# Reading the moving operand of float32r matmuls in pairs of columns 128 apart

## The chip, the cores and the metric

The kernel runs on one core of a Trainium2 chip. The metric is the device time of one execution in microseconds. The profile is one execution taken by the hardware profiler; its times are counted from the first instruction's start.

## The reference

A linear attention feeds a two-layer network, all in float32. Batch 8, 8 heads, sequence 576, head width 64, so 4608 tokens of width 512; the inner width of the network is 2048.

```python
kv  = np.einsum('bhsd,bhse->bhde', k, v)
o   = np.einsum('bhsd,bhde->bhse', q, kv)
rms = np.sqrt(np.mean(o * o, axis=-1, keepdims=True) + 1e-06)
x   = (o / rms * g_norm).transpose(0, 2, 1, 3).reshape(4608, 512)
h   = x @ w_in                                   # 4608 x 2048
g   = 0.5 * h * (1.0 + erf(h / np.sqrt(2.0)))
out = g @ w_out                                  # 4608 x 512
```

The weights w_in and w_out arrive as float64 and are handed over as 64-bit words.

## The kernel before

The tokens are worked through in nine chunks of 512. In every chunk the attention output x stands transposed, features on the partitions and tokens along the free dimension; layer 1 gives h transposed in the same way, and layer 2 takes the Gelu of it as stationary operand, so that its output has tokens on the partitions and the 512 features of the result along the free dimension.

To keep float32 precision with float32r matmuls, each operand is split into a high part (rounded to float32r) and the low rest, and a product is made of three matmuls: high by high, low by high, high by low. A float32r matmul has a stationary operand of 128 x 128 and a moving one of 256 or 512 columns; each loads its stationary operand first.

Chunks 0 and 1 are done plainly. `layer1` (L680) makes 12 matmuls of 512 columns for each of the 16 blocks of 128 inner features; the first two blocks of chunk 0 are plain float32 matmuls of 256 columns (L670) because their split weights aren't ready. `layer2` (L707) makes 12 matmuls of 512 columns for each block. In the same time VectorE and ScalarE turn the 64-bit words of the weights into split float32r parts (`top_w`, L635; `bits_w`, L645 and L648; `high_w`, L656; `low_w`, L660), form sums of weight blocks, and store these to HBM.

Chunks 2 to 8 use a fast scheme with seven products of half-sized blocks in the place of eight, for both layers. `product` (L569) makes six matmuls of 256 columns for one product of layer 1, and 56 products in a chunk; `Fast.matmuls` (L1257) makes 12 matmuls of 256 columns for each of 28 ticks of layer 2. Weight sums come back from HBM through a ring of six tiles (`RING`, `fetch`, L513 and L518): the tile is fetched again as soon as its last matmul has read it, and a fetch holds the operands of 12 matmuls. Some sums stay resident.

Queries of the next chunk are projected by plain float32 matmuls with 64 x 64 weights (`project_pair`, L243), four or more for each pair of heads, between the other matmuls of TensorE. `sum_squares` (L836) belongs to the first chunk alone: it streams 64 columns of a table against 128-column stationary blocks in plain float32. All instruction order is written out by hand. SyncE's queue issues the transfers.

In the code before, the moving operands are adjacent columns in memory. The pieces of them, in `product`, `layer1`, `layer2` and `Fast.matmuls`:

```python
rhs=x[:, z, kb]
rhs=at.block((p // 2, half))[:, p % 2]
rhs=at.x[p][:, x]
rhs=parts["out", i][:, w]
rhs=y
```

`finish` is defined and called from nowhere.

Of the kernel before, what the change touches and what calls it, by code (L numbers as in the profile page):

```python
# [8 lines left out]
F32 = mybir.dt.float32  # L9
F32R = mybir.dt.float32r  # L10
I32 = mybir.dt.int32
AF = mybir.ActivationFunctionType
ALU = mybir.AluOpType
# [3 lines left out]
P = 128  # L17
EPS = 1e-6
CH = 512
# [5 lines left out]
HALF = CH // 2  # L25
# [12 lines left out]
def linear_attn_rms_gelu_ffn(  # L38
# [16 lines left out]
    nc = tc.nc  # L55
    ctx.enter_context(tc.manual_schedule())
    NT, DM = out.shape
    B, NP = kv_main.shape[:2]
    S = NT // B
    NJ = kv_main.shape[3] // (2 * P)  # L60
    TAIL = kv_tail.shape[1]
    D = g_norm.shape[0]
# [6 lines left out]
    work = ctx.enter_context(tc.tile_pool(name="work", bufs=1))  # L69
# [4 lines left out]

    def bank(name):
        return psum.tile([P, 512], F32, name=name)

    turn = {"h": 0, "a": 0}

    def next_bank(kind):  # L80

        turn[kind] ^= 1
        return bank(f"{kind}{turn[kind]}")

    kv = [const.tile([P, NP, 2, D], F32, name=f"kv{s}") for s in range(2)]
# [91 lines left out]
    def rows(r):  # L177
        return slice(r * D, (r + 1) * D)
# [26 lines left out]
    class Attn:  # L205
# [22 lines left out]
        def project_pair(self, p):  # L228


            q = self.q.pop(p).rearrange("p (h n) -> p h n", h=2)
            parts = []
            for half in range(2):
                a, t = 0, self.t0 + half * HALF
                while a < HALF:
                    b = (t + a) // S
                    e = min(HALF, (b + 1) * S - t)
                    parts.append((a, e, half, b))
                    a = e
            for a, e, half, b in sorted(parts):  # L240
                ps = self.ps[p // 2, half]
                for h in range(2):
                    nc.tensor.matmul(  # L243
                        out=ps[rows(h), p % 2 * HALF + a:p % 2 * HALF + e],
                        lhsT=kv[b % 2][rows(half), p, h ^ half], rhs=q[rows(half), h, a:e],
                        start=True, stop=True,
                    )

# [313 lines left out]
    def product(at, j, k, out, first=False):  # L562
        *key, n = place_in(j, k)
        key = tuple(key)
        w, x = operand(at.c, key)[n], at.x[k]
        for kb in range(2):
            hi, lo = (w[:, m * HALF + kb * P:m * HALF + (kb + 1) * P] for m in range(2))
            for i, (y, z) in enumerate(((hi, 0), (lo, 0), (hi, 1))):
                nc.tensor.matmul(  # L569
                    out=out, lhsT=y, rhs=x[:, z, kb], start=first and kb + i == 0,  # L570
                    stop=kb == 1 and i == 2, skip_group_check=True,
                )
        if (n == 1) or (k == 6 and j == NJ2 - 1):
            used(at.c, key)
# [40 lines left out]
    raw, parts = {}, {}  # L615
# [49 lines left out]
    def layer1(at, i):  # L665
        h = next_bank("h")
        if at.c == 0 and i < FULL:
            for half in range(2):
                for p in range(NP):
                    nc.tensor.matmul(  # L670
                        out=h[:, half * HALF:(half + 1) * HALF],
                        lhsT=ws[i].bitcast(F32)[:, p * P:(p + 1) * P],
                        rhs=at.block((p // 2, half))[:, p % 2],
                        start=(p == 0), stop=(p == NP - 1),
                    )
            return h
        order = ((HI, 0), (LO, 0), (HI, 1))
        for m, (w, x) in enumerate(order):
            for p in range(NP):
                nc.tensor.matmul(  # L680
                    out=h, lhsT=parts["in", i][:, w][:, p * P:(p + 1) * P], rhs=at.x[p][:, x],
                    start=(m + p == 0), stop=(m == 2 and p == NP - 1),
                )
        return h
# [17 lines left out]
    def layer2(acc, blocks, closed=None):  # L702
        for t, ps in enumerate(acc):
            ts = slice(t * P, (t + 1) * P)
            for (gh, gl), i in blocks:
                for m, (x, w) in enumerate(((gh, HI), (gh, LO), (gl, HI))):
                    nc.tensor.matmul(  # L707
                        out=ps, lhsT=x[:, ts], rhs=parts["out", i][:, w],
                        start=(i == 0 and m == 0),
                        stop=(m == 2 and (i == NF - 1 or (i, t) == (closed, CH // P - 1))),  # L710
                    )

    def finish(acc, blocks, t0):


        layer2(acc[:-1], blocks)
        store(acc[:-1], t0)
        t = len(acc) - 1
        ts, rows = slice(t * P, (t + 1) * P), slice(t0 + t * P, t0 + (t + 1) * P)
        rest_ps = next_bank("h")  # L720
        for half in range(2):
            ps = rest_ps[:, :HALF] if half else acc[t][:, :HALF]
            n = 0
            for (gh, gl), i in blocks:
                for x, w in ((gh, 0), (gh, DM), (gl, 0)):
                    w += half * HALF
                    n += 1
                    nc.tensor.matmul(
                        out=ps, lhsT=x[:, ts], rhs=parts["out", i][:, w:w + HALF],
                        start=(half == 1 and n == 1), stop=(n == 3 * len(blocks)),  # L730
                        skip_group_check=True,
                    )
            o = work.tile([P, DM], I32, name="wz"[half], bufs=2).bitcast(F32)[:, :HALF]
            if half:
                nc.vector.tensor_copy(out=second_half, in_=acc[t][:, HALF:])
                nc.vector.tensor_tensor(out=o, in0=ps, in1=second_half, op=ALU.add)
            else:
                second_half = work.tile([P, CH], F32, name="sq")[:, :HALF]
                nc.scalar.copy(out=o, in_=ps)
            nc.sync.dma_start(out=out[rows, half * HALF:(half + 1) * HALF], in_=o)  # L740

    def store(acc, t0, both=True, to=None):
        for t, ps in enumerate(acc):
            if to is None:
                o = work.tile([P, DM], I32, name="wz"[t % 2], bufs=2).bitcast(F32)
            else:
                o = to[:, t]
            if both and not t % 2:
                nc.vector.tensor_copy(out=o, in_=ps)
            else:  # L750
                nc.scalar.copy(out=o, in_=ps)
            nc.sync.dma_start(out=out[t0 + t * P:t0 + (t + 1) * P, :], in_=o)
# [3 lines left out]
    first, second = attn[:2]  # L756
# [44 lines left out]
    for d in range(0, 2 * D, BLK):  # L801
        h = d // D * D
        nc.gpsimd.tensor_tensor(
            out=fold[:, d:d + BLK], in0=ident[:, h:h + BLK], in1=ident[:, h + BLK:h + 2 * BLK],
            op=ALU.add,
        )
    SQ = ("sq", "gh", "gl", "gh")
    sq, NG = {}, CH // P
# [23 lines left out]
    def sum_squares(n):  # L832
# [9 lines left out]
    ps = next_bank("a")  # L842
    nc.tensor.matmul(out=ps[:, :1], lhsT=g_row, rhs=heads[:1, :1], start=True, stop=True)
    nc.vector.tensor_scalar(
        out=half_g, in0=ps[:, :1], scalar1=0.5, scalar2=None, op0=ALU.mult
# [3 lines left out]
        out=sums[:, :P], lhsT=ones, rhs=eps, start=True, stop=False,  # L849
        skip_group_check=True,  # L850
# [3 lines left out]
        out=root_g, in0=half_g, scalar1=D ** 0.5, scalar2=None, op0=ALU.mult  # L854
# [9 lines left out]
    for half in range(2):  # L864
# [6 lines left out]
        out=sums[:, :n_fold].rearrange("p (g b) -> p g b", g=2), lhsT=fold,  # L871
# [22 lines left out]
    for half in range(2):  # L894
# [6 lines left out]
        n = 2 + half  # L901
# [296 lines left out]
    class Fast:  # L1198
# [44 lines left out]
        def matmuls(self, i, sides=(0, 1)):  # L1243
            k, n = self.ticks[i]
            name = self.BANKS[k]
            two = self.c == NCH - 1 and name == "a0"
            if k in (0, 2, 1) and n == 0 and 0 in sides:
                self.bank[name] = [bank(name), bank("a1")] if two else [bank(name)] * 2
            w = operand(self.c, ("out", k, n))
            slot, op = self.ops[i]  # L1250
            for p in range(2):
                hi, lo = (op[:, z * CH + p * HALF:z * CH + (p + 1) * HALF] for z in range(2))
                wh, wl = (w[p][:, m * HALF:(m + 1) * HALF] for m in range(2))
                for a in sides:
                    at = slice(a * P, (a + 1) * P)
                    for m, (x, y) in enumerate(((hi, wh), (hi, wl), (lo, wh))):
                        nc.tensor.matmul(  # L1257
                            out=self.bank[name][a][:, a * HALF:(a + 1) * HALF],
                            lhsT=x[:, at], rhs=y,
                            start=(k in (0, 2, 1) and n + p + m == 0 and (two or a == 0)),  # L1260
                            stop=(n == GROUPS - 1 and p == 1 and m == 2), skip_group_check=True,
                        )
            if 1 in sides:
                used(self.c, ("out", k, n))
                free.append(slot)
                self.ops.pop(i)
# [208 lines left out]
```

## Time and profile before

| what | value |
|---|---|
| time, median of 3 runs | 772.47 us (771.27 to 773.56) |
| span of the profiled execution, first to last instruction | 769.2 us |
| TensorE busy | 762.4 us, 99% of the span |
| VectorE, ScalarE, GpSimd busy | 75%, 48%, 20% |
| DMA | 244.90 MB, 318 GB/s mean |

The time of a run lies 2.1 to 4.4 us above the span of the profiled execution, since it takes in what stands before the first and after the last instruction; the profiled execution itself has no other time than its span. A matmul's duration in the profile is that from its start until its last result, and starts follow one another before the one ahead has ended; the pace of a run of matmuls is the distance of their starts.

### The profile page before, as it was taken

How to read it: one execution, taken by the hardware profiler on the slowest of the kernel's cores; microseconds unless marked ns; L12 is line 12 of the kernel's file. 1: busy time of each engine (PE TensorE's matmuls, PEld its weight loads, DVE VectorE, ACT ScalarE, POOL GpSimd, SP SyncE). 2: the span in 40 equal slices, each digit the busy share in tenths (PEclk: the TensorE clock that was granted, in tenths of full speed). 3: DMA queues.
4: the chain of work that ended last, by engine and by line, in shares of the span. 5: the costliest groups of instructions: out<-in, count | busy, mean ns of one | idle time of the engine just before them, and what ended most of it. 6: DMA issues, size and time to landing. Idle time of an engine off the chain costs nothing.

```text
span 769.2 us, 16747 instructions
## 1 busy us (share of the span) xinstructions
PE 762.4 (99%) x6558; PEld 721.4 (94%) x6558; DVE 575.8 (75%) x1056; ACT 369.4 (48%) x722; POOL 156.3 (20%) x140
## 2 busy tenths in 40 slices
PE   8999999999999999999999999999999999999998
PEld 6888888888899999999999999999999999999998
DVE  3999979899668965688477947694689577954683
ACT  3777635534364635364435624471446254622460
POOL 1000126423517000800062004400250026001100
PEclk9999999999999999999999999999999999999999
DMA  9997973797999999979999999989898989799974
GB/s 349 406 408 256 372 261 145 272 358 260 344 312 361 382 339 339 377 266 369 347 356 309 332 357 334 340 283 350 297 333 275 357 309 326 246 324 341 338 249 157
DMA packets 91618, 244.90 MB, mean 318 GB/s; under 512 B 9108, under 2 KB 31124, under 8 KB 91540
## 3 DMA queue, kind: packets, MB, share of 16 engines
q1 hardware_dynamic: 91536, 243.83, 88.0%
q8 instruction: 52, 0.85, 0.5%
q14 instruction: 26, 0.21, 0.1%
q10 hardware_dynamic: 4, 0.00, 0.0%
HBM read 207.09 MB, written 34.08 MB: 314 GB/s over the span
## 4 chain that ended last, share of the span: by engine, by line
PE 98%; DMA 1%; DVE 0%; ACT 0%; issue 0%; ACTq 0%
PE acc L1257 25%; PE acc L569 22%; PE h L569 13%; PE acc L707 11%; PE h L680 11%; PE a L1257 10%; PE a L190 2%; DMA w_out<-kv_main 1%; PE a L243 1%; PE h L670 1%; PE acc L243 1%; PE h L836 0%; PE acc L905 0%; DVE t L319 0%; ACT gh L886 0%
## 5 line engine op out<-in xcount | busy, mean ns | idle before, releaser
L336 POOL TENSOR_TENSOR o<-o,sq 128x512 f32<-128x512 f32 x23 | 31.2, 1356 | 321.2 <-PE acc L569 247.5
L680 PE MATMUL h<-x,w_in 128*128 128x512 f32 x360 | 86.9, 390 | 0.0
L680 PEld LDWEIGHTS h<-x,w_in 128*128 128x128 f32 x360 | 67.3, 188 | 14.5 <-issue 0.3
L707 PE MATMUL acc<-w_out,gh 128*128 128x512 f32 x256 | 79.3, 391 | 0.0
L569 PE MATMUL acc<-w_in,w_in 128*128 128x256 f32 x480 | 64.2, 277 | 0.0
L569 PEld LDWEIGHTS acc<-w_in,w_in 128*128 128x128 f32 x480 | 58.8, 188 | 0.3 <-issue 0.2
L707 PEld LDWEIGHTS acc<-w_out,gh 128*128 128x128 f32 x256 | 47.7, 188 | 10.2 <-issue 0.4
L569 PE MATMUL acc<-x,w_in 128*128 128x256 f32 x390 | 52.3, 278 | 0.0
L560 DVE TENSOR_TENSOR gl<-acc,gh 128x256 f32<-128x256 f32 (+1 forms) x77 | 34.2, 445 | 22.1 <-ACT gh L582 17.8
L707 PE MATMUL acc<-w_out,gl 128*128 128x512 f32 x128 | 49.8, 389 | 0.0
L693 ACT ACTIVATE gh<-h 128x512 fp32r<-128x512 f32 x32 | 19.1, 597 | 62.5 <-PE h L680 62.4
L569 PEld LDWEIGHTS acc<-x,w_in 128*128 128x128 f32 x390 | 47.8, 188 | 1.0 <-issue 0.8
L582 ACT COPY gh<-h 128x256 f32<-128x256 f32 x21 | 7.8, 369 | 84.0 <-PE h L569 84.0
L1257 PE MATMUL acc<-w_in,w_in 128*128 128x256 f32 x372 | 46.6, 277 | 0.0
L1257 PEld LDWEIGHTS acc<-w_in,w_in 128*128 128x128 f32 x372 | 44.3, 188 | 0.0
L1257 PE MATMUL acc<-w_in,x 128*128 128x256 f32 x324 | 40.5, 277 | 0.0
L1257 PEld LDWEIGHTS acc<-w_in,x 128*128 128x128 f32 x324 | 38.5, 188 | 0.1
L569 PE MATMUL h<-w_in,w_in 128*128 128x256 f32 x288 | 38.5, 276 | 0.0
L601 ACT ACTIVATE w_in<-acc 128x512 f32<-128x512 f32 x32 | 19.2, 599 | 39.4 <-DVE acc L560 39.4
L285 DVE TRANSPOSE_TENSOR_REDUCE part<-sq 128x16 f32<-128x512 f32 x33 | 23.4, 708 | 17.6 <-ACT sq L275 17.6
L569 PEld LDWEIGHTS h<-w_in,w_in 128*128 128x128 f32 x288 | 35.3, 188 | 0.0
L1257 PE MATMUL acc<-w_in,w_out 128*128 128x256 f32 x264 | 32.9, 276 | 0.0
(302 smaller groups left out, 1883.6 us busy)
## 6 DMA issues: line engine op xcount, KB each, us to landing
w_in<-products_in SPq DMA_DIRECT2D x161, 512.0 KB, 5.3
w_in<-products_out SPq DMA_DIRECT2D x126, 512.0 KB, 5.1
products_in<-w_in SPq DMA_DIRECT2D x40, 256.0 KB, 5.2
w_in<-w_in SPq DMA_DIRECT2D x16, 512.0 KB, 10.2
w_out<-w_out SPq DMA_DIRECT2D x16, 512.0 KB, 10.1
q<-qT SPq DMA_DIRECT2D x15, 512.0 KB, 6.9
kv_main<-kv_main SPq DMA_DIRECT2D x14, 512.0 KB, 6.7
products_out<-w_out SPq DMA_DIRECT2D x23, 256.0 KB, 5.2
```

The costliest lines, as they stand in the source:

```text
L190: nc.tensor.matmul(out=ps[r, n * D:(n + 1) * D], lhsT=k[:, r], rhs=v[:, r], start=(j == 0), stop=(j == NJ),)
L243: nc.tensor.matmul(out=ps[rows(h), p % 2 * HALF + a:p % 2 * HALF + e], lhsT=kv[b % 2][rows(half), p, h ^ half], rhs=q[rows(half), h, a:e], ...
L285: nc.vector.tensor_reduce(out=self.part[:, 2 * k[0] + k[1], :], in_=sq.rearrange("p (b d) -> p b d", d=BLK), op=ALU.add, axis=AX.X, apply_ ...
L336: eng.tensor_tensor(out=o, in0=o, in1=bc, op=ALU.mult)
L560: return eng.tensor_tensor(out=out, in0=x, in1=y, op=op)
L569: nc.tensor.matmul(out=out, lhsT=y, rhs=x[:, z, kb], start=first and kb + i == 0, stop=kb == 1 and i == 2, skip_group_check=True,)
L582: nc.scalar.copy(out=u[:, left], in_=a[:, left])
L601: nc.scalar.activation(out=grid(t)[:, :, j % 2], in_=ps.rearrange("p (a n) -> p a n", a=2), func=AF.Gelu)
L680: nc.tensor.matmul(out=h, lhsT=parts["in", i][:, w][:, p * P:(p + 1) * P], rhs=at.x[p][:, x], start=(m + p == 0), stop=(m == 2 and p == NP ...
L693: nc.scalar.activation(out=gh, in_=h, func=AF.Gelu)
L707: nc.tensor.matmul(out=ps, lhsT=x[:, ts], rhs=parts["out", i][:, w], start=(i == 0 and m == 0), stop=(m == 2 and (i == NF - 1 or (i, t) == ...
L1257: nc.tensor.matmul(out=self.bank[name][a][:, a * HALF:(a + 1) * HALF], lhsT=x[:, at], rhs=y, start=(k in (0, 2, 1) and n + p + m == 0 and ...
```

## The change

Where a float32r matmul read its moving columns as 0, 1, 2, ..., it reads them as 0, 128, 1, 129, ...: pairs of columns 128 apart, from a block of 256. A 512-column operand is two such blocks. The matmul writes its output columns in adjacent places as before. So that the results come out in the right order, the data stand the other way round in memory: of each 256 columns, the even ones come first and the odd ones after them. For the token columns that begins with the queries, which are laid out so on the host; the projection keeps this order in what it writes. For the features of the second layer it begins with w_out, laid out so on the host. Work between them is done column by column or in whole blocks, and stays as it was. The plain float32 matmuls of L670 are read in the same way, and the projection, still plain float32, now reads and writes two runs of columns 128 apart. `finish` is removed.

```diff
+    def woven(t):
+        if t.shape[-1] == HALF:
+            return t.rearrange("p (a n) -> p n a", a=2)
+        return t.rearrange("p (h a n) -> p h n a", h=2, a=2)
...
-            q = self.q.pop(p).rearrange("p (h n) -> p h n", h=2)
+            q = self.q.pop(p).rearrange("p (h z n) -> p h z n", h=2, z=2)
...
-                ps = self.ps[p // 2, half]
+                at = slice(a // 2, e // 2)
+                ps = self.ps[p // 2, half].rearrange("p (g z n) -> p g z n", g=2, z=2)[:, p % 2]
...
-                        out=ps[rows(h), p % 2 * HALF + a:p % 2 * HALF + e],
-                        lhsT=kv[b % 2][rows(half), p, h ^ half], rhs=q[rows(half), h, a:e],
+                        out=ps[rows(h), :, at],
+                        lhsT=kv[b % 2][rows(half), p, h ^ half], rhs=q[rows(half), h, :, at],
...
-                    out=out, lhsT=y, rhs=x[:, z, kb], start=first and kb + i == 0,
+                    out=out, lhsT=y, rhs=woven(x[:, z, kb]), start=first and kb + i == 0,
...
-                        rhs=at.block((p // 2, half))[:, p % 2],
+                        rhs=woven(at.block((p // 2, half))[:, p % 2]),
...
-                    out=h, lhsT=parts["in", i][:, w][:, p * P:(p + 1) * P], rhs=at.x[p][:, x],
+                    out=h, lhsT=parts["in", i][:, w][:, p * P:(p + 1) * P],
+                    rhs=woven(at.x[p][:, x]),
...
-                        out=ps, lhsT=x[:, ts], rhs=parts["out", i][:, w],
+                        out=ps, lhsT=x[:, ts], rhs=woven(parts["out", i][:, w]),
...
-    def finish(acc, blocks, t0):
...
-                            lhsT=x[:, at], rhs=y,
+                            lhsT=x[:, at], rhs=woven(y),
...
-            q.transpose(1, 3, 0, 2).reshape(NP // 2, 2, 2, D, B * S // CH, 2, CH // 2)
-            .transpose(4, 0, 5, 3, 1, 2, 6)
+            q.transpose(1, 3, 0, 2).reshape(NP // 2, 2, 2, D, B * S // CH, 2, CH // 4, 2)
+            .transpose(4, 0, 5, 3, 1, 2, 7, 6)
...
-        "w_out": lay(moe_w_out.view(np.int64)),
+        "w_out": lay(
+            moe_w_out.view(np.int64).reshape(DF, 2, DM // 4, 2).transpose(0, 1, 3, 2)
+        ).reshape(DF, DM),
```

## Rows read from the trace of the kernel before

**Rows 1.** The page: span, busy time of engines, tenths in 40 slices.

```profile
span 769.2 us, 16747 instructions
...
PE 762.4 (99%) x6558; PEld 721.4 (94%) x6558; DVE 575.8 (75%) x1056; ACT 369.4 (48%) x722; POOL 156.3 (20%) x140
...
PEclk9999999999999999999999999999999999999999
```

**Rows 2.** The page: the chain that ended last, by engine and line.

```profile
PE 98%; DMA 1%; DVE 0%; ACT 0%; issue 0%; ACTq 0%
PE acc L1257 25%; PE acc L569 22%; PE h L569 13%; PE acc L707 11%; PE h L680 11%; PE a L1257 10%; PE a L190 2%; DMA w_out<-kv_main 1%; PE a L243 1%; PE h L670 1%; PE acc L243 1%; PE h L836 0%; PE acc L905 0%; DVE t L319 0%; ACT gh L886 0%
```

**Rows 3.** Windows of the span: busy us of each engine, clock, DMA.

```profile
core 0: us, PE busy (x) PEld busy (x) DVE busy (x) ACT busy (x) POOL busy (x), PEclk, DMA share, GB/s
0.00:27.00 27.00, 23.43 (x237) 19.32 (x238) 14.72 (x37) 13.11 (x26) 2.19 (x15) 1.00 0.95 365
27.00:112.00 85.00, 85.00 (x515) 69.64 (x514) 75.09 (x131) 56.66 (x106) 8.96 (x8) 1.00 0.96 348
112.00:206.00 94.00, 94.00 (x525) 77.52 (x524) 85.59 (x130) 44.34 (x86) 38.26 (x34) 1.00 0.73 260
206.00:769.00 563.00, 559.93 (x5288) 554.90 (x5286) 400.40 (x760) 255.34 (x506) 106.86 (x84) 1.00 0.90 321
```

**Rows 4.** Timeline of PE, merged runs: start us, length us, instruction, count.

```profile
180.81 2.88 PE L680 MATMUL h<-x,w_in 128*128 128x512 f32 x12
...
440.87 4.24 PE L1257 MATMUL acc<-w_in,w_in 128*128 128x256 f32 x36
...
22.87 4.70 PE L670 MATMUL h<-o,w_out 128*128 128x256 f32 x21
...
15.42 1.08 PE L836 MATMUL h<-heads,gh 128*128 128x64 f32 x8
```

**Rows 5.** Groups by line and shape: xcount | busy us, mean ns | idle.

```profile
L680 PE MATMUL h<-x,w_in 128*128 128x512 f32 x360 | 86.9, 390 | 0.0
...
L1257 PE MATMUL acc<-w_in,w_in 128*128 128x256 f32 x372 | 46.6, 277 | 0.0
...
L670 PE MATMUL h<-o,w_out 128*128 128x256 f32 x32 | 7.3, 382 | 0.0
```

**Rows 6.** Weight loads of L836: the timeline's run, and the group.

```profile
15.39 0.97 PEld L836 LDWEIGHTS h<-heads,gh 128*128 128x128 f32 x8
...
L836 PEld LDWEIGHTS h<-heads,gh 128*128 128x128 f32 x8 | 1.0, 192 | 0.0
```

**Rows 7.** Whole span, one line each: L569, L1257, L680, L707, L243.

```profile
0.00:769.20 769.20, 270.93 (x2352) 268.41 (x2352) 1.00 0.89 318
...
0.00:769.20 769.20, 268.40 (x2352) 267.58 (x2352) 1.00 0.89 318
...
0.00:769.20 769.20, 86.86 (x360) 67.34 (x360) 1.00 0.89 318
...
0.00:769.20 769.20, 92.78 (x384) 71.69 (x384) 1.00 0.89 318
...
0.00:769.20 769.20, 20.03 (x384) 13.77 (x384) 1.00 0.89 318
```

**Rows 8.** Waits of SP's queue: waited for, us in total, times, longest.

```profile
SPq L518 <- PE acc L569: 131.6, 99, 3.9
SPq L518 <- PE acc L1257: 106.5, 81, 5.0
SPq L518 <- PE h L569: 57.2, 56, 2.7
SPq L518 <- PE a L1257: 40.0, 38, 2.3
```

**Rows 9.** DMA issues: tensors, count, KB each, median us to landing.

```profile
w_in<-products_in SPq DMA_DIRECT2D x161, 512.0 KB, 5.3
w_in<-products_out SPq DMA_DIRECT2D x126, 512.0 KB, 5.1
```

**Rows 10.** ScalarE's and VectorE's groups of the weight conversion, 27 to 112 us.

```profile
L635 ACT ACTIVATE z<-w_out 128x512 f32<-128x512 f32 x15 | 10.1, 673 | 0.3 <-DMA w_out<-w_out 0.3
L656 ACT CAST w_out<-w 128x512 fp32r<-128x512 f32 x15 | 9.2, 613 | 2.4 <-DVE w L648 2.3
...
L648 DVE SCALAR_TENSOR_TENSOR w<-w_out,w 128x512 int32<-128x512 int32 x15 | 10.4, 692 | 0.5
...
L660 DVE TENSOR_TENSOR w_out<-w,w_out 128x512 fp32r<-128x512 f32 x15 | 10.3, 683 | 0.0
```

More of the change, by code (lines that the diff above doesn't have):

```diff
@@ L711, in layer2 @@
                     )
-    def finish(acc, blocks, t0):
[L716 to L740, printed above, removed]
     def store(acc, t0, both=True, to=None):
```

## The prediction

> **What bounds the kernel now.** [...] The chain that ended last [rows 2] is TensorE for 98% of the span; four lines of float32r matmuls, L1257, L569, L707 and L680, carry it. Busy is no proof of peak speed, so the next question is how far apart their starts are. The windows [rows 3] show that no idle time is left: from 27 us on, TensorE's row has no gap except a few us near the end.
>
> The spacing comes from the merged runs of the timeline [rows 4]; a run of n equal matmuls lasts n-1 spacings and one duration, and durations are in [rows 5]. Twelve 512-column matmuls of L680 take 2.88 us: (2.88 - 0.390) / 11 = 226.4 ns each. Thirty-six 256-column ones of L1257 take 4.24 us: (4.24 - 0.277) / 35 = 113.2 ns. [...]
>
> [...] The plain float32 matmuls of L670 (256 columns, 32 records for the 16 matmuls in the code) have 21 in 4.70 us: (4.70 - 0.382) / 20 = 216 ns. [...] The change alters the order of the reading and nothing else.
>
> [...]
>
> **The change, part by part.** The float32r matmuls [rows 7]: L680 has 360 and L707 384, together 744 of 512 columns; L569 and L1257 have 2352 each, 4704 of 256. Count, sizes, weights, order and outputs stay. Their duration under the new reading isn't in this trace. [...]
>
> [...] For 512 columns I use the 216 ns that L670 needs for 512 clocks of stream: 744 x 10.4 ns = 7.7 us. For 256 columns the stream would need 109.4 ns by the same 2.7 ns, but the weight-load floor of 111.1 is later: 4704 x 2.1 ns = 9.9 us. Sum 17.6 us. So the 256-column matmuls, three quarters of the work, gain 1.9%, the 512-column ones 4.6%.
>
> [...]
>
> What could be late next: VectorE is busy 75.1 of the 85 us to 112 and 85.6 of 94 to 206 [rows 3]. The 7.7 us come out of these stretches, so it would be at 92 and 95%. It is hidden behind TensorE today, with no TensorE wait to be seen; if that cover failed, at most the 7.7 us would be lost again. I deduct nothing. For the operands fetched from HBM, the queue waits for TensorE to release a tile [rows 8], so a faster TensorE starts fetches earlier. Six tiles of 12 matmuls each turn round in 6 x 12 x 113.2 ns = 8.2 us and a fetch lands in 5.3 us or less at the median [rows 9]; 2.1 ns less per matmul takes 0.15 us of the 2.9 left.
>
> The projections (L243, 384 records, 20.0 us of busy time [rows 7]) stay plain float32 and now read and write two runs of half the length, 128 apart. Runs of 32 to 128 adjacent columns should cost nothing. If every spacing doubled, it would be up to the 20 us; I take 0. L670 (32 x 216 ns = 6.9 us) is woven too: 0, at most 6.9 us. The new layouts of the queries and of w_out are made before the launch; the transfers move the same number of rows of the same size, so 0. `finish` is never called: 0.
>
> The span becomes 769.2 - 17.6 = 751.6 us. The median of the runs shown is 772.5, 3.3 above the profiled span, and I add these: 755 us.
>
> **The rivals.**
>
> *A step to another place costs each time (slower).* Today four adjacent columns stand in 16 bytes; woven, each is 512 bytes from the one before. If the read path holds only the last place, every column is a new fetch. [...] Against it: reads of every second 4-byte word (L635 on ScalarE, L648 on VectorE) last 673 and 692 ns against 613 and 683 for adjacent words (L656, L660) [rows 10]: 10% and 1%, no doubling; but they never leave a 16-byte piece after one word. Chance 0.27, two thirds of it for the steep form.
>
> [...]
>
> [...] Chance 0.16.
>
> *The weight load is no floor for float32r (much faster).* L836 is plain float32, whose loads may differ. [...] Chance 0.17.
>
> **How the numbers follow.** The forecast has 0.40: a single change to the read, priced by the floors that the trace shows. Its own range is 749 to 768: the lower end if the floor is a little lower, the upper if VectorE or the projections take most of the 512-column gain. Faster by over 0.3% (which is about what runs from 771.3 to 773.6 can tell) is the forecast and the last rival, 0.57; the same 0.16; slower 0.27. The range for 8 in 10 reaches from 728, with the whole loss gone, through no change, up to 800, which takes in about a third of the slow rival.
>
> **What would show it.** Right: runs of L680 spaced near 216 ns, of L1257 and L569 near 111, weight loads 111 apart, L243 and L670 unchanged, TensorE still without gaps. 226 and 113 again would mean that the order doesn't matter; 109 or less in L1257, that weight loads are no floor; 216 or more in L1257, that each step costs. L680 faster and L1257 unchanged would mean that the weight load is what spaces the 256-column ones already. A new wait of TensorE on VectorE before 206 us, or on a fetch after it, would mean a step that I costed at nothing.

## The result and the profile after

The changed kernel takes 760.76 us (median of 4 runs, 759.13 to 762.75), the kernel before 772.04: a ratio of 0.9858, 95% interval 0.9837 to 0.9878, or 11.3 us less. The forecast was 755 us.

Line numbers move: L680 of before is now L687, L707 is L715, L569 is L576, L1257 is L1236, L670 is L677. First the page, beside [rows 1, 2]:

```profile
span 758.9 us, 16747 instructions
PE 750.3 (99%) x6558; PEld 715.2 (94%) x6558; DVE 580.6 (77%) x1056; ACT 374.3 (49%) x722; POOL 154.2 (20%) x140
...
PE 77%; DVE 9%; DMA 7%; ACT 4%; issue 3%; SPq 1%; DVEq 0%; ACTq 0%
```

TensorE is as busy as before by share, but its part of the chain has fallen from 98% to 77%: the chain now runs for a stretch through VectorE, ScalarE and the transfers of raw weights. VectorE is busy 4.8 us longer although its 1056 instructions are the same. Then the timeline of TensorE, beside [rows 4]: start, length, instruction, count.

```profile
178.74 2.75 PE L687 MATMUL h<-x,w_in 128*128 128x512 f32 x12
...
181.32 0.59 PE L715 MATMUL acc<-w_out,gh 128*128 128x512 f32 x2
182.27 0.48 PE L715 MATMUL acc<-w_out,gl 128*128 128x512 f32 x1 [0.35 <-DVE gl L707]
...
22.18 8.45 PE L677 MATMUL h<-o,w_out 128*128 128x256 f32 x30
...
435.74 4.07 PE L1236 MATMUL acc<-w_in,w_in 128*128 128x256 f32 x35
```

TensorE's waits from 20 to 206 us, which are waited for, us in total, times and longest:

```profile
PE acc L715 <- DVE gl L707: 1.5, 4, 0.5
```

With a duration of 0.380 us (the page's group of L687), twelve 512-column matmuls are (2.75 - 0.38) / 11 = 215.5 ns apart, where they were 226.4. Thirty-five of 256 columns are (4.07 - 0.275) / 34 = 111.6 ns apart, where they were 113.2. The plain float32 matmuls of L677 went the other way: the median distance of their starts is 273 ns, where it was 216 (the first distance of the run shown, 363 ns, falls partly into a stretch with a granted clock of 0.50, of which more below). And L715 waits for VectorE's low part of the Gelu, which the kernel before shows nowhere after 27 us: four waits, 1.5 us of visible idle time. The time lost is longer than the idle time, because a matmul still shows as busy for 0.38 us when its successor could have started after 0.216: L715 at 182.27 shows 0.35 us of idle time and starts 0.52 us later than two spacings behind 181.32, where the two matmuls ahead of it begin. By the distances of starts, five such waits (one too short for the list) cost 2.3 us, and the matmuls right behind them 0.5.

Where the 10.3 us between the two profiled spans come from can be read from starts of the timeline, here those of the kernel before and then of the changed one:

```profile
31.66 1.52 PE L680 MATMUL h<-x,w_in 128*128 128x512 f32 x6
205.27 0.40 PE L569 MATMUL h<-x,w_in 128*128 128x256 f32 x2
...
34.84 1.46 PE L687 MATMUL h<-x,w_in 128*128 128x512 f32 x6
203.36 0.83 PE L576 MATMUL h<-x,w_in 128*128 128x256 f32 x6
```

A step is the work on one of the 16 blocks of inner features in a plain chunk, counted from 0. Steps 0 and 1 of the first chunk have the plain float32 matmuls, so the 512-column matmuls of layer 1 begin with step 2, called the second step below, at 31.66 us before and 34.84 after. The fast chunks begin at 205.27 and 203.36, and the end is at 769.2 and 758.9. The start lost 3.2 us, the plain chunks won 5.1, the fast chunks 8.4.

### The profile page after: what moved, and what is told of

Its sections match the earlier page's. It is cut to its first block, busy times and chain, and to the rows that moved or that the text cites. A ratio compares the mean times of both kernels' runs of the same rounds, so it can differ in the third digit from the quotient of the medians.

```text
span 758.9 us, 16747 instructions
## 1 busy us (share of the span) xinstructions
PE 750.3 (99%) x6558; PEld 715.2 (94%) x6558; DVE 580.6 (77%) x1056; ACT 374.3 (49%) x722; POOL 154.2 (20%) x140
## 4 chain that ended last, share of the span: by engine, by line
PE 77%; DVE 9%; DMA 7%; ACT 4%; issue 3%; SPq 1%; DVEq 0%; ACTq 0%
PE acc L1236 24%; PE acc L576 21%; PE h L576 12%; PE a L1236 10%; DMA w_out<-w_out 4%; PE acc L715 4%; PE h L687 3%; PE a L196 2%; DMA kv_main<-kv_main 1%; DVE gl L707 1%; PE a L250 1%; ACT z L642 1%; DVE w L652 1%; DMA w_in<-qT 1%; DVE w L454 1%
## 5 line engine op out<-in xcount | busy, mean ns | idle before, releaser
L687 PE MATMUL h<-x,w_in 128*128 128x512 f32 x360 | 82.9, 380 | 0.0
L687 PEld LDWEIGHTS h<-x,w_in 128*128 128x128 f32 x360 | 67.8, 189 | 10.1 <-issue 0.3
L715 PE MATMUL acc<-w_out,gh 128*128 128x512 f32 x256 | 76.6, 381 | 0.0
L576 PE MATMUL acc<-w_in,w_in 128*128 128x256 f32 x480 | 63.4, 276 | 0.0
L576 PEld LDWEIGHTS acc<-w_in,w_in 128*128 128x128 f32 x480 | 58.2, 192 | 0.3 <-issue 0.2
L715 PEld LDWEIGHTS acc<-w_out,gh 128*128 128x128 f32 x256 | 48.0, 189 | 7.0 <-issue 0.4
L576 PE MATMUL acc<-x,w_in 128*128 128x256 f32 x390 | 51.4, 276 | 0.0
L715 PE MATMUL acc<-w_out,gl 128*128 128x512 f32 x128 | 49.0, 383 | 1.5 <-DVE gl L707 1.5
L576 PEld LDWEIGHTS acc<-x,w_in 128*128 128x128 f32 x390 | 47.1, 192 | 1.0 <-issue 0.8
L1236 PE MATMUL acc<-w_in,w_in 128*128 128x256 f32 x372 | 45.8, 275 | 0.0
L1236 PEld LDWEIGHTS acc<-w_in,w_in 128*128 128x128 f32 x372 | 43.6, 192 | 0.0
L701 ACT ACTIVATE gh<-h 128x512 fp32r<-128x512 f32 x32 | 19.0, 594 | 45.5 <-PE h L687 45.0
L1236 PE MATMUL acc<-w_in,x 128*128 128x256 f32 x324 | 39.9, 275 | 0.0
L576 PE MATMUL h<-w_in,w_in 128*128 128x256 f32 x288 | 38.0, 275 | 0.0
L1236 PEld LDWEIGHTS acc<-w_in,x 128*128 128x128 f32 x324 | 37.9, 192 | 0.1
L576 PEld LDWEIGHTS h<-w_in,w_in 128*128 128x128 f32 x288 | 35.0, 192 | 0.0
L1236 PE MATMUL acc<-w_in,w_out 128*128 128x256 f32 x264 | 32.4, 275 | 0.0
```

The lines of the kernel that those rows point to most:

```text
L576: nc.tensor.matmul(out=out, lhsT=y, rhs=woven(x[:, z, kb]), start=first and kb + i == 0, stop=kb == 1 and i == 2, skip_group_check=True,)
L687: nc.tensor.matmul(out=h, lhsT=parts["in", i][:, w][:, p * P:(p + 1) * P], rhs=woven(at.x[p][:, x]), start=(m + p == 0), stop=(m == 2 and ...
L701: nc.scalar.activation(out=gh, in_=h, func=AF.Gelu)
L715: nc.tensor.matmul(out=ps, lhsT=x[:, ts], rhs=woven(parts["out", i][:, w]), start=(i == 0 and m == 0), stop=(m == 2 and (i == NF - 1 or (i ...
L1236: nc.tensor.matmul(out=self.bank[name][a][:, a * HALF:(a + 1) * HALF], lhsT=x[:, at], rhs=woven(y), start=(k in (0, 2, 1) and n + p + m == ...
```

## The experiments

### Each half of the change

```diff
 e1_only_512: product, Fast.matmuls and the float32 matmuls of layer1
-                    rhs=woven(...)
+                    rhs=...
 e2_only_256: layer1 and layer2
-                    rhs=woven(...)
+                    rhs=...
```

> Only the 744 matmuls of 512 columns (L687, L715) read in pairs 128 apart; the 4704 of 256 columns and the 32 plain float32 ones read adjacent columns, so the order of tokens and features in the results is not the reference's. [...] Rival (the gain is a side effect of other addresses or of the new layout, not of the reading order): about 761 us as the changed kernel, and 256 columns at 112.

> The other half: only the 4704 matmuls of 256 columns read in pairs, the 512-column and the plain float32 ones read adjacent columns, so the order of tokens and features in the results is not the reference's. My theory: 256 columns at 111 to 112 ns, 512 at 226.4, no wait of TensorE on VectorE before 206 us, a gain of about 8 us, some 764 us. Rival as before: the same time as the changed kernel, or as before it. The two gains together should be about that of the changed kernel plus the 1.8 us that its float32 matmuls lose.

Measured: 767.49 us for the 512-column half (0.9950, interval 0.9935 to 0.9965) and 763.08 for the 256-column half (0.9891, 0.9875 to 0.9908), against 771.5 before. In each kernel only the lines that read in pairs changed pace: 216 ns with 113 in the first, 227 with 112 in the second (medians of the distances of starts), and the float32 matmuls are back at 216 in both. The new layout is in both kernels, so it is the reading order that does it. The two gains, 4.0 and 8.4 us, make 12.4. With the 1.8 us of the float32 matmuls, which neither half bears, the changed kernel's 11.3 would have made 13.1. TensorE waits 2.7 us for VectorE from 20 to 206 us in the first kernel and not at all in the second, so these waits come with the paired reading of the 512-column matmuls.

### Which order

```diff
 e3_orders: layer1 in chunk 1
-                    rhs=woven(at.x[p][:, x]),
+                    rhs=read(at.x[p][:, x]),     # read = ORDERS[i], one for each step
```

> The 12 matmuls of layer 1 in each of the 16 steps of the second chunk read their 512 columns in 16 different orders, one for each step (the token order of these results is not the reference's). Steps in turn: adjacent; pairs 128 apart; pairs 256 apart; pairs 64, 32, 16, 8, 4 and 2 apart; 4, 8, 32 and 128 streams; runs of 2, 4 and 16 adjacent columns taken in turn from the two halves. Theory 1 (a column's fetch is late only when the read moves on to the next 16 words; any two places at least 16 words apart hide it): 216 ns for pairs 16 and more apart and for 4 to 32 streams, 226 for adjacent and for pairs 2 to 8 apart. Theory 2 (two banks told apart by the address bit of 512 bytes): 216 only for pairs 128 apart, 226 or more for pairs 256 apart and all others. [...]

The timeline shows the 12 matmuls of each step, in the order of the list (the first is adjacent columns, the next eight are pairs 128, 256, 64, 32, 16, 8, 4 and 2 apart):

```profile
112.53 2.90 PE L699 MATMUL h<-x,w_in 128*128 128x512 f32 x12
117.86 2.75 PE L699 MATMUL h<-x,w_in 128*128 128x512 f32 x12
123.04 2.75 PE L699 MATMUL h<-x,w_in 128*128 128x512 f32 x12
...
151.39 2.75 PE L699 MATMUL h<-x,w_in 128*128 128x512 f32 x12
156.57 2.90 PE L699 MATMUL h<-x,w_in 128*128 128x512 f32 x12
161.90 3.56 PE L699 MATMUL h<-x,w_in 128*128 128x512 f32 x12
167.89 6.03 PE L699 MATMUL h<-x,w_in 128*128 128x512 f32 x12
...
192.26 4.24 PE L699 MATMUL h<-x,w_in 128*128 128x512 f32 x12
198.93 3.16 PE L699 MATMUL h<-x,w_in 128*128 128x512 f32 x12
204.52 3.04 PE L699 MATMUL h<-x,w_in 128*128 128x512 f32 x12
```

The row at 151.39 is pairs 4 apart, and the steps between it and 123.04 last 2.75 us too. So every distance tried from 4 to 256 columns gives 216 ns, and pairs 2 apart, which stay inside four adjacent columns, give the 227 of adjacent ones. Theory 1 fits the pairs with another border (between 2 and 4 columns, not at 16) and fails for the streams, for which it had 216; theory 2 is out. (n streams: the operand is cut into n pieces of equal length, and one column is taken from each in turn.) Of the numbers tried, two is the best: four streams take 283 ns, eight 487, 32 and 128 streams 432 and 461 (medians); runs of 2, 4 and 16 columns from two places 340, 246 and 240. So going to a place 4 or more columns away at every column costs nothing in the pairs that were tried (216 ns), and in the four or more streams a matmul takes at least 67 ns longer (283 and up). What in the read path makes it so isn't shown.

### The weight load as a floor

```diff
 e4_floor: product and Fast.matmuls, five of each six matmuls (in short)
-                    out=out, lhsT=y, rhs=woven(x[:, z, kb])
+                    out=out[:m, :n], lhsT=y[:, :m], rhs=x[:, z, kb][:, :n]   # woven or not, by chunk
```

> In the fast chunks 3 to 7 the last five of each six matmuls are narrowed (that part of the products is left out): chunk 3 streams 128 adjacent columns, chunk 4 128 columns in pairs, chunk 5 has 64-column weights with 256 adjacent columns, chunk 6 the same in pairs, chunk 7 is full size but adjacent; chunks 2 and 8 are as in the changed kernel. My theory (a load of 128 columns of weights sets a floor of 111 ns): 111 ns in chunks 3 and 4 although half the columns stream, 113.2 in chunk 5 and 7, and in chunk 6, with the floor at about half, 109.4 or less. Rival 1 (no floor, the stream alone counts): 55 to 60 ns in chunks 3 and 4, 112 in chunk 6. [...]

The timeline of layer 1 in chunk 4 (sixes: one full matmul, five of 128 columns), its weight loads, and chunk 6 (five of each six with 64 columns of weights; the form printed is that of the first):

```profile
365.87 0.83 PE L587 MATMUL h<-w_out,w_in 128*128 128x256 f32 x6
366.54 0.83 PE L587 MATMUL h<-x,w_in 128*128 128x256 f32 x6
367.21 0.83 PE L587 MATMUL h<-w_in,w_in 128*128 128x256 f32 x6
...
366.48 0.75 PEld L587 LDWEIGHTS h<-x,w_in 128*128 128x128 f32 x6
367.15 0.75 PEld L587 LDWEIGHTS h<-w_in,w_in 128*128 128x128 f32 x6
...
526.73 0.82 PE L587 MATMUL h<-w_in,w_in 128*128 128x256 f32 x6
527.39 0.82 PE L587 MATMUL h<-s,w_in 128*128 128x256 f32 x6
```

The same line with adjacent columns, in chunk 3 (five of each six with 128 columns) and in chunk 5 (64 columns of weights):

```profile
300.37 0.84 PE L587 MATMUL h<-w_in,w_in 128*128 128x256 f32 x6
301.05 1.52 PE L587 MATMUL h<-x,w_in 128*128 128x256 f32 x12
...
460.07 0.84 PE L587 MATMUL h<-w_in,w_in 128*128 128x256 f32 x6
460.75 1.52 PE L587 MATMUL h<-x,w_in 128*128 128x256 f32 x12
```

In chunk 4 a six starts 0.67 us after the one ahead, 112 ns a matmul: taking away nearly half of the columns wins nothing, and the loads are 112 ns apart (0.67 / 6). With 64 columns of weights and the full stream it is 0.66 us, and the median distance in that chunk is 109 ns, in layer 2 as well. That is the 109.4 that the prediction had for the stream alone. In chunk 5, 64 columns of weights under adjacent reading leave 113 to 114 (0.68 us a six). So the floor of 111 to 112 ns is the weight load's, which rules out rival 1. And adjacent reading stays slower, 113 to 114 ns against 109, when the loads have half the columns, so the loads aren't what makes it slower.

Two numbers fit nothing. In chunk 3, where half the columns stream and the loads should set 111 to 112 ns, adjacent reading takes 0.68 us a six, 113 ns a matmul, so the order of reading counts a little there too. And in chunk 7, full size with adjacent columns, layer 1 ran at 118 ns, not 113.

```diff
 g3_chunks_adjacent: product
-                    rhs=woven(x[:, z, kb])
+                    rhs=x[:, z, kb] if at.c in (4, 7) else woven(x[:, z, kb])
```

> The changed kernel, but layer 1 of the fast chunks 4 and 7 reads adjacent columns (the token order of these results is not the reference's). It asks where the 118 ns of chunk 7 in the floor experiment came from. If adjacent reading costs 113 ns wherever the chunk before it was not narrowed: 113 in both, and the 118 belong to what ran ahead of it. If adjacent reading in chunk 7 meets the weight loads in another way than in the kernel before: 118 in chunk 7 again.

Measured: 118 ns in both chunks, 112 in the others; in e1, where all chunks read adjacent columns, it is 113 in all. The narrow chunk ahead is not the reason. What is stays open, so 113 ns for adjacent columns is the pace of the kernels that read so throughout, and not of every kernel.

### The start, and what it is worth

> The changed kernel once more, beside the three others of this set on one chip. Expected 760 to 762 us, and a profile that shows whether the late first 27 us (the second step's first 512-column matmul at 34.8 us against 31.7) belong to the kernel or to the execution: of these 3.2 us the 1.8 of L677 must come back in each profile, the rest, which follows a wait for a transfer of keys, may not.

The same kernel again: 759.32 us (0.9844, 0.9830 to 0.9857), below the range expected, span 757.3. Its second step's first L687 starts at 33.14 us, 1.5 after the kernel before, and L677 is at 273 ns again. The remaining 1.7 us of the first profile's late start belong to that execution. Part of it, 0.65 us, stands behind waits for transfers of keys (the same matmuls of L196 start at 18.83 and 18.18 us). Then its granted clock is 0.50 from 19.0 to 22.4 us, where the second profile has 1.00 over the first 27 us; what lowered it isn't shown.

```diff
 f3_stride_out: layer1, float32 matmuls
-                        out=h[:, half * HALF:(half + 1) * HALF],
+                        out=h[:, half * HALF:(half + 1) * HALF].rearrange("p (n a) -> p a n", a=2),
-                        rhs=woven(at.block((p // 2, half))[:, p % 2]),
+                        rhs=at.block((p // 2, half))[:, p % 2].rearrange("p (a n) -> p a n", a=2),
 f4_at_gelu: the same matmuls
-                        rhs=woven(at.block((p // 2, half))[:, p % 2]),
+                        rhs=at.block((p // 2, half))[:, p % 2],
 and in gelu, for these two blocks
+            nc.scalar.activation(out=gh4, in_=woven(h), func=AF.Gelu)
```

> The changed kernel, but the 32 plain float32 matmuls (L670 of before) read adjacent columns and write every second output column, so the result stays in token order. My theory: they are back at 216 ns for 273 if the write's step costs nothing, which wins 1.8 us against the changed kernel. Rival (a step of two in PSUM slows the write): 273 ns or more, up to 2 times, no gain or up to 7 us lost.

> The changed kernel, but the 32 plain float32 matmuls read and write adjacent columns, so the two blocks that they make stand in the order even columns first, and the Gelu of these two blocks reads them in pairs 128 apart (so does the subtraction for the low part). Expected: 216 ns again for the 32 matmuls, and two ScalarE and two VectorE instructions longer by at most their own length, 0.6 us each, off TensorE's path: 1.8 us won, some 759 us. Rival (the start of the kernel waits for other things anyway): the same time as the changed kernel.

Both bring the float32 matmuls back to a median of 216 ns, so a step of two in what they write costs nothing. Neither wins time: 759.37 (0.9845, 0.9832 to 0.9859) and 759.52 (0.9847, 0.9833 to 0.9860). In f4 the second step starts at 31.68 us, 1.5 ahead of f1; by the first L576 it is at 202.15 against 201.73. TensorE's waits for VectorE have grown from 1.5 to 2.8 us of visible idle time. The first plain chunk is paced by VectorE, and the 1.8 us of both expectations aren't won.

### Why VectorE is late

```diff
 f2_relief: convert (and the same in sum_weights), late steps
+            if i > 8 and not k:
+                gelu_rest()
             if n is not None:
                 bits_w(n)
-            if i and not k:
+            if 0 < i < 9 and not k:
                 gelu_rest()
 g1_both: f2 and f4 together
 g2_offload: g1, and in steps 2 to 8 of chunk 0
-                low_w(last.pop())
+                low_w(last.pop(), nc.gpsimd)     # first of each step
```

> The changed kernel, but in the later steps of the two plain chunks VectorE computes the low part of the Gelu before the weight work of that step and no longer behind it. My theory (the missing 2.4 us of the plain chunks are TensorE's waits for that low part, because VectorE is now nearly full there): the waits of L715 on L707 vanish and 1.5 to 2.5 us are won against the changed kernel, some 758.5 us. Rival (VectorE is full, so any order makes something else late): the waits move to weights and the time stays at 761.

> The earlier low part of the Gelu together with the Gelu that reads in pairs for the two float32 blocks. My theory after the last set (VectorE paces the first plain chunk, so a start that is 1.5 us earlier is lost again in waits for it unless VectorE's order is mended as well): with both, 1 us or more is won beyond the 758.2 of the earlier low part alone, 756.5 to 757.5 us. Rival (VectorE's amount of work and not its order is the limit): 758 us.

> The same, and in steps 2 to 8 of the first chunk one subtraction of the weight conversion in each step is done by GpSimd, which is idle there. If VectorE's amount of work is what is left (7 x 0.68 = 4.8 us less on it): TensorE's waits before 113 us vanish and the second chunk starts up to 1 us earlier than without it, 756 us. Rival (GpSimd, at about 1.3 us for such a piece, is late with it and slows VectorE's instructions beside it): no gain or a loss of 1 to 3 us.

f2 takes 758.24 us (0.9829, 0.9815 to 0.9842): 1.1 us less than f1 beside it (its five runs, 757.98 to 758.29, all lie below f1's four, 759.10 to 759.61), and less than the 1.5 to 2.5 expected. Its waits of TensorE from 20 to 206 us are

```profile
PE h L687 <- ACT x L355: 0.5, 1, 0.5
PE acc L715 <- DVE gl L707: 0.3, 1, 0.3
```

so most of those for VectorE are gone and one for ScalarE is new. g1 adds nothing (759.02 us; 0.9828, 0.9811 to 0.9846), as its rival had it: VectorE's order is not all. g2 loses (760.55; 0.9848, 0.9828 to 0.9868), as its rival had it: with GpSimd at work beside it, VectorE's L655 lasts 1101 ns, where the changed kernel has 828. What else had changed on VectorE gives the answer. The groups of the weight conversion from 27 to 112 us in the changed kernel, beside [rows 10]:

```profile
L642 ACT ACTIVATE z<-w_out 128x512 f32<-128x512 f32 x15 | 13.1, 872 | 0.0
...
L663 ACT CAST w_out<-w 128x512 fp32r<-128x512 f32 x15 | 9.2, 613 | 3.3 <-DVE w L655 3.1
...
L655 DVE SCALAR_TENSOR_TENSOR w<-w_out,w 128x512 int32<-128x512 int32 x15 | 12.4, 828 | 0.5
...
L667 DVE TENSOR_TENSOR w_out<-w,w_out 128x512 fp32r<-128x512 f32 x15 | 10.1, 676 | 0.0
```

L642 and L655 read every second word of the raw weights. They last 872 and 828 ns where they lasted 673 and 692. Those that read adjacent words, L663 and L667, last no longer than before. In e1 L655 lasts 848 ns, in e2 692, L642 there 676. It comes with the paired reading of the 512-column matmuls, which run at the same time.

```diff
 h1_contend: layer1 and layer2 in chunk 0
-                    rhs=woven(...)
+                    rhs=reads(c, i)(...)     # by two steps: pairs 128 apart twice, adjacent, 256, 4, 16, 64
```

> Found after the sets before: while the 512-column matmuls read in pairs, the two conversion instructions that read every second word of the raw weights last longer (ScalarE's of top_w 674 to 870 ns, VectorE's second of bits_w 692 to 830), and not in the kernel whose 512-column matmuls read adjacent columns. Here the matmuls of the first chunk change their order every two steps: pairs 128 apart in steps 0 to 3, adjacent in 4 and 5, pairs 256 apart in 6 and 7, 4 apart in 8 and 9, 16 apart in 10 and 11, 64 apart from 12 on (tokens and features of that chunk don't stand in the reference's order). [...] Theory 2 (two places 512 or 1024 bytes apart share a bank, near places don't): 870 and 830 up to step 3 and in 6 and 7, near 674 and 692 in steps 8 to 11.

ScalarE's and VectorE's group in four windows of this kernel: steps with pairs 128 apart (34 to 44 us), adjacent (45.5 to 54.8), 256 apart (57 to 66.5), 4 and 16 apart (68.5 to 87). ScalarE's row for the last is that of w_in: in the four windows w_in has 817, 675, 833 and 676 ns, w_out 892, 674, 898 and 700.

```profile
L652 ACT ACTIVATE z<-w_out 128x512 f32<-128x512 f32 x2 | 1.8, 892 | 0.0
L665 DVE SCALAR_TENSOR_TENSOR w<-w_out,w 128x512 int32<-128x512 int32 x3 | 2.5, 837 | 0.1
...
L652 ACT ACTIVATE z<-w_out 128x512 f32<-128x512 f32 x3 | 2.0, 674 | 0.0
L665 DVE SCALAR_TENSOR_TENSOR w<-w_out,w 128x512 int32<-128x512 int32 x2 | 1.4, 692 | 0.1
...
L652 ACT ACTIVATE z<-w_out 128x512 f32<-128x512 f32 x2 | 1.8, 898 | 0.0
L665 DVE SCALAR_TENSOR_TENSOR w<-w_out,w 128x512 int32<-128x512 int32 x3 | 2.5, 843 | 0.1
...
L652 ACT ACTIVATE z<-w_in 128x512 f32<-128x512 f32 x4 | 2.7, 676 | 0.0
L665 DVE SCALAR_TENSOR_TENSOR w<-w_out,w 128x512 int32<-128x512 int32 x4 | 2.8, 692 | 0.1
```

Pairs 4 and 16 apart, at which TensorE runs at 216 ns (e3), leave the other engines at 676 to 700 and 692 ns; with pairs 128 and 256 apart ScalarE's last 817 to 898 ns and VectorE's 830 to 843. So it isn't reading in pairs alone that slows them: the distance counts. The pattern of theory 2 holds; that a shared bank is behind it is not shown. The kernel took 757.98 us in its one run (span 756.1), 771.24 for the kernel before beside it, although two of its steps read adjacent columns. A kernel with pairs 16 apart throughout was not run.

TensorE's waits from 20 to 206 us in h1, and VectorE's from 27 to 112 us in the kernel before and in the changed one:

```profile
PE acc L725 <- DVE gl L717: 0.7, 2, 0.4
...
DVE gl L699 <- ACT h L694: 6.1, 4, 4.6
...
DVE gl L707 <- ACT h L702: 0.5, 1, 0.5
```

Both waits of h1 stand behind 178 us, in the second chunk. The two listed waits of the first chunk (at 100 and 111 us in the changed kernel) are gone, so the longer conversion brought them, as far as one run can show; its two adjacent steps also give VectorE some 0.5 us (48 x 11 ns). The second and third row tell how: before, VectorE stood idle for 6.1 us because its input wasn't there yet, and in the changed kernel this reserve is used up. Late by then, it meets GpSimd too. Before and after:

```profile
89.68 0.22 DVE L319 SCALAR_TENSOR_TENSOR y<-t,y 128x64 f32<-128x64 f32 x1
92.65 3.00 POOL L560 TENSOR_TENSOR s<-w_out 128x512 f32<-128x512 f32 x2 [88.05 <-ACT h L694]
...
93.36 2.58 POOL L567 TENSOR_TENSOR s<-w_out 128x512 f32<-128x512 f32 x2 [88.76 <-DVE t L326]
94.82 1.20 DVE L326 SCALAR_TENSOR_TENSOR y<-t,y 128x64 f32<-128x64 f32 x1
```

The five instructions of this line took 1.1 us together when they ran ahead of GpSimd's work, and 4.0 when all but the first ran beside it. The two waits of the second chunk are another matter: the conversion is over there and they stay in h1. What brings them was not tested.

## Why the prediction was right, and where it was off

- **The order of reading sets the pace.** Shown, by e1, e2 and e3: the order alone moves it (227 to 216 and 113 to 112 ns). The rival of a cost at each step is wrong for two places taken in turn (216 ns, against 227 for adjacent columns) and right in kind for four or more streams (283 to 487 ns). That adjacent columns took 118 ns in two runs stays unexplained, and so does what in the reading costs the time.
- **512 columns at 216 ns.** That 512 float32r columns need what 256 plain float32 ones do was the author's estimate; no run shows the 512 clocks behind it. Measured for the 512 columns in pairs: 215.5 to 216.
- **256 columns at the floor of the weight load.** Shown by e4: the floor exists, at 111.6 to 112 ns for the forecast 111.1, which is the distance of the loads in [rows 6], (0.97 - 0.192) / 7. No run shows the 2.7 ns that the forecast 109.4 holds; with loads of 64 columns the stream takes 109. The mean distance of starts fell from 114.0 to 112.1 ns in layer 1 and from 113.6 to 112.0 in layer 2, for the forecast 2.1: 2352 x (1.9 + 1.6) ns = 8.2 us of the 9.9.
- **The float32 matmuls, costed at 0 with up to 6.9 us.** Measured 32 x 57 ns = 1.8 us, of which f3 and f4 show that nothing is to be had while VectorE paces the chunk. They show that the reading makes it; why the order that helps float32r harms plain float32 is open.
- **The projections, costed at 0 with up to 20 us.** L250, which was L243, has 384 records and 20.0 us of busy time, as before.
- **VectorE, costed at nothing.** This is the step that failed. The 30 steps from the second on should have won 7.5 us (720 x 10.4 ns); they won 5.1 and 5.0 in the two profiles. The prediction saw a fuller VectorE in a shorter stretch, and bounded the loss at 7.7 us, which holds. What it did not see is that VectorE's and ScalarE's work would grow: 29 x about 130 ns and 28 x about 190 ns in the first chunk, 3.8 and 5.3 us, beside TensorE's paired reads. With the instructions that then run beside GpSimd, 2.9 us longer for the five of L326, VectorE rose from 75.1 to 81.1 of the 85 us to 112. About half of TensorE's idle time in these waits (0.8 of 1.5 us) stands in the first chunk, where h1 has none; for the other half, in the second, the cause is open.
- **The fetches.** As costed: after 206 us TensorE waits for none (once for VectorE, 0.2 us), and the ring's median landing is 5.4 us for 5.3.

So 17.6 us forecast less 1.5 in the fast chunks, 2.5 in the plain chunks' waits for VectorE and 1.5 to 3.2 at the start leave 10.4 to 12.1, beside the 10.3 and 11.9 by which the two spans are shorter. The time stayed inside the forecast's own range for the reason given for its upper half: VectorE took part of the 512-column gain.

Two numbers of the prediction don't follow. The 3.3 us added to the span compare a median with the span of another execution; each run lies 1.8 to 2.0 us above its own span, which would have made 753.5 of the 755. And no run shows the whole loss that the 728 at the foot of its wide range takes as gone: the shortest spacing measured is 109 ns for 256 columns, 4 less than with adjacent ones, and 215.5 for 512, 11 less.

## What to carry to other kernels

When an engine is busy all the time, compare runs of different length and of different rate: the spacing that doubled with the columns here (113.2 and 226.4 ns) belonged to the stream, and hung on the order in which it reads. Before counting a gain, look for the next floor on the same engine; here the weight load left 1.6 ns of the 4.2 that the stream gave with lighter loads (113.2 to 111.6 and to 109). And when an edit changes how one engine reads, compare the durations of the other engines' unchanged instructions, group by group, before blaming their order: two groups out of four had grown by 20 and 30%.

## What the runs showed of the hardware

A float32r stream of adjacent columns runs at 113.2 and 226.4 ns for 256 and 512 columns (118 for 256 in two kernels, unexplained). Taken in turn from two places, it runs at 109 for 256 columns (128 apart, weights of 64 columns) and at 216 for 512 (every distance tried from 4 to 256 columns). Loads of 128 columns of weights follow one another 111 to 112 ns apart. Plain float32 matmuls of 256 columns get slower by the same reading, 216 to 273 ns, and not by writing every second column (216). Reads by ScalarE and VectorE with a step of two words are slowed (673 to 872 and 692 to 828 ns) beside a paired read of TensorE 128 and 256 columns apart, and not 4 or 16 apart (676 to 700 and 692).
